# Logits of a fused attention and soft-MoE kernel as four wide products and four that add them up, with permuted features and two more weight buffers

## The chip, the cores and the metric

The kernel runs on one core of one Trainium2 chip. The metric is the device time of one execution in microseconds (us). Everything is in float32.

## The reference, cut to what matters

```python
# attention: q, k, v are (4, 8, 768, 64); 24 chunks of 32 queries; each sees 8 memory rows and up to 56 keys
for c in range(nc):
    k_full = concatenate([mem_k, k[:, :, l_start:r_end]], axis=2)     # 16 rows left of the chunk, 8 right of it
    scores = scale * matmul(q_c, k_full.T)
    a = exp(scores - max); a = a / (sum(a) + 1e-09)
    out[:, :, c_start:c_end] = matmul(a, v_full)
x = out.transpose(0, 2, 1, 3).reshape(3072, 512)                      # tokens x features
# soft MoE: 8 experts with 4 slots each, hidden size 1024
logits = x @ phi                                                      # 3072 x 32
d = softmax of logits over the tokens
slot_input = d.T @ x                                                  # 32 x 512
slot_out[e] = relu(slot_input[e] @ w1[e]) @ w2[e]
c = softmax of logits over the slots
return c @ slot_out
```

## The kernel before, in words

Attention works on 12 units (`u`) of 256 tokens, all heads. For each unit TensorE computes the scores (`s`, 64 rows of the trace: every float32 product is two), transposes the exponentials (`pt_ps`, 8), multiplies them with the values (`a`, 64), and transposes the normalized result x (`xt_ps`, 8) into xT, in which the features lie on the partitions. A loop over `i` writes the order of all engines by hand: transposes of x of unit i - 1, exponent of unit i + 1, values of unit i, scores of unit i + 2, transposes of the exponentials of unit i + 1. Two units make a group G of four 128-token blocks. In even iterations the logits of group (i - 2) / 2 follow the values: 16 products (32 rows), one for each of four feature sets of 128 (`kc`) and each of four blocks, accumulated over kc on four column groups of 32. Right behind normalizing, VectorE takes their maximum (`dispatch_max`) and ScalarE their exponential (`dispatch_exp`). In odd iterations the exponentials are transposed (`dt_ps`) and multiplied with x (`D_ps`, 8 rows of 512 columns), and VectorE adds the result to D_sb.

VectorE takes maxima, subtracts, sums and normalizes; ScalarE takes exponentials and copies transposes out of PSUM; GpSimd copies columns of k and rows of v. All loads are issued by SyncE, in program order: q two units ahead, k three buffers, v four and three buffers, and between them the experts' weights in 32 pieces of 1 MB (`load_w`). A piece goes to one of 8 buffers of its own (`w`) or to a buffer of attention that is free by then (three of k, one of q, five of v, two of x): 19 in all. `freed` lists from which half iteration each may be used. Piece i lies in buffer i modulo their number, so piece 19 waits until the experts have read piece 0.

After the loop comes a bridge of small steps: the last group's logits, the transposes of the maxima, the last D_ps, the slot inputs (`si_ps`, four products that read D_sb with a step of 4 elements, since feature p * 4 + kc belongs on partition p for w1), with filling products (`fill`) between them. Then the experts: `h` (first layer), `ht_ps`, `so` (second layer, in two halves of the output columns), `r`, and `o` (combination), whose results are copied and written out.

In front of the first scores stand 8 warming products of 128 columns, behind them 3 more.

Of the kernel before, what the change touches and what calls it, by code (L numbers as in the profile page):

```python
# [10 lines left out]
F32 = mybir.dt.float32  # L11
# [24 lines left out]
E = 8  # L36
# [16 lines left out]
WLAST = 7  # L53
WARM0 = 8
WARM1 = 3
FILL = (3, 2, 4, 1, 3, 2)
# [18 lines left out]
def tile_attn_softmoe(  # L75
# [17 lines left out]
    k_t = [cp.tile([P, 2, KW], F32, tag=f"k{i}", name=f"k{i}") for i in range(NB)]  # L93
    v_t = cp.tile([P, NE + NO, 2, VW], F32, tag="v", name="v")
    x_t = [cp.tile([P, 4, DM], F32, tag=f"x{i}", name=f"x{i}") for i in range(2)]
    w_slab = [cp.tile([P, PIECE], F32, tag=f"w{i}", name=f"w{i}") for i in range(NW)]
    lT = cp.tile([P, NG, P], F32, tag="lT", name="lT")
    late = [v_t[:, at].rearrange("p a n -> p (a n)") for at in (NE + (NU - 1) % NO, (NU - 1) % NE)]
    hT = late[0].rearrange("p (e f s) -> p e f s", e=E, s=NSLOT)
    c_sb = late[1][:, 0:4 * NG * NSLOT].rearrange("p (u s) -> p u s", s=NSLOT)  # L100
    cst = [late[1][:, 4 * NG * NSLOT + P * G:4 * NG * NSLOT + P * G + P] for G in range(NG)]
    D_sb = cp.tile([P, DM], F32, tag="D", name="D_sb")
# [42 lines left out]

    def even_v(u):

        return v_t[:, u % NE]

    def odd_v(u):  # L150
        return v_t[:, NE + u % NO]

    def load_v(u):
# [20 lines left out]
    freed += [(2 * NU - 5, q_t.rearrange("p a g n -> p (a g n)"))]  # L174
    freed += [(2 * u, even_v(u).rearrange("p a n -> p (a n)")) for u in range(NU - NE, NU - 1)]
    freed += [(2 * u, odd_v(u).rearrange("p a n -> p (a n)")) for u in range(NU - NO, NU - 1)]
    freed += [(2 * NU + d, x_t[(NG + d) % 2].rearrange("p u n -> p (u n)")) for d in range(2)]
    usable = {i: NW for i in range(2 * NU + 2)}
# [48 lines left out]
    first_k(2)  # L227
    w_ps = row(P, "warm_ps")

    def keep_warm(n, tile=None):  # L230
        for _ in range(n):
            pe.matmul(w_ps if tile is None else tile, lhsT=warm, rhs=warm, start=True, stop=True)

    keep_warm(WARM0)

    pexp, rz, xT = {}, {}, {}

# [10 lines left out]

    def scores(u, parts=1):

        if parts == 1:
            tiles = [banks(f"s{u}", "S")]
        else:
            tiles = [row(512, f"s{u}_{s}").rearrange("p (s n) -> p s n", s=1) for s in range(NSUB)]
        tiles = [t.rearrange("p s (g h n) -> p s g h n", g=NPAIR, h=2) for t in tiles]
        for s in range(NSUB):
            t, at = (tiles[0], s) if parts == 1 else (tiles[s], 0)
            for g in range(NPAIR):  # L260
                for j in range(4):
                    pe.matmul(
                        t[32 * j:32 * j + 32, at, g],
                        lhsT=q_t[:, u % NQ, g, P * s + 32 * j:P * s + 32 * j + 32],
                        rhs=key_columns(u, 4 * s + j, g),
                        start=True, stop=True,
                    )
        return tiles

    def softmax(u, tiles):  # L270
        mx = wk.tile([P, 16, 1], F32, tag="mx", name=f"mx{u}")
        p = pexp[u] = wk.tile([P, 8, 4 * CHUNK], F32, tag="p", name=f"p{u}")
        step = NSUB // len(tiles)
# [58 lines left out]
    def normalize(u, a_ps):  # L332
        dve.tensor_tensor(
            out=x_of(u).rearrange("p s (m d) -> p (s m) d", d=D),
            in0=a_ps.rearrange("p s g h d -> p (s g h) d"),
            in1=rz[u].broadcast_to([P, 16, D]),
            op=ALU.mult,
        )

    def transpose_x(u):  # L340
        for s in range(NSUB):
            t_ps = row(512, f"xt_ps{u}_{s}")
            for kc in range(NKC):
                pe.transpose(t_ps[:, P * kc:P * kc + P], x_of(u)[:, s, P * kc:P * kc + P], ident)
            xT[2 * u + s] = wk.tile([P, NKC, P], F32, tag="xT", name=f"xT{u}_{s}", bufs=4)
            act.copy(out=xT[2 * u + s].rearrange("p g n -> p (g n)"), in_=t_ps)

    def logits(G):
        l_ps = row(P, f"l{G}")
        for kc in range(NKC):  # L350
            for g in range(4):
                pe.matmul(
                    l_ps[32 * g:32 * g + 32, :],
                    lhsT=phi_sb[:, kc, :],
                    rhs=xT[4 * G + g][:, kc, :],
                    start=(kc == 0), stop=(kc == NKC - 1),
                )
        return l_ps
# [12 lines left out]
    def dispatch_exp(G, l_ps):  # L371
        d = wk.tile([P, P], F32, tag="d", name=f"d{G}")
        act.activation(out=d, in_=l_ps, func=AF.Exp, bias=nmx[G], scale=1.0, accum_out=zg[G])
        dexp[G] = d
        if G:
            act.activation(out=alpha[G], in_=nmx[G - 1], func=AF.Exp, bias=nmx[G], scale=-1.0)

    def dispatch_t(G):
        t_ps = row(P, f"dt_ps{G}")
        pe.transpose(t_ps, dexp[G], ident)  # L380
        dT[G] = wk.tile([P, P], F32, tag="dT", name=f"dT{G}")
        act.copy(out=dT[G], in_=t_ps)
# [21 lines left out]
    s0 = scores(0, 2)  # L404
    keep_warm(WARM1)
    softmax(0, s0)
# [17 lines left out]
    for i in range(NU):  # L424
# [11 lines left out]
        if G is not None and first:  # L436
            l_ps = logits(G)
        if G is not None and not first:
# [4 lines left out]
        load_w(int(WRATE * (i + 0.5)) if i < WLAST else usable[2 * i])  # L443
        if G is not None and first:
            dispatch_max(G, l_ps)
            dispatch_exp(G, l_ps)
        if G is not None and not first:
            dispatch_z(G)
            dispatch_sum(G)
        if i + 2 < NU:  # L450
            softmax(i + 2, scores(i + 2))
        if i + 1 < NU:
# [46 lines left out]
    si_ps = row(NKC * NSLOT, "si_ps").rearrange("p (c s) -> p c s", c=NKC)  # L499
    D_v = D_sb.rearrange("p (n kc) -> p kc n", kc=NKC)  # L500
    for kc in range(NKC):
# [82 lines left out]
    def expert_out(blk):  # L584
        o_ps = banks(f"so{blk}", "S")[:, 0, 0:WB]
        for e in range(E):
# [9 lines left out]
            load_w(len(slabs) + 2 * E + E * blk + e + 1)  # L596
        so = wk.tile([P, WB], F32, tag="xT", name=f"so_sb{blk}", bufs=4)
        dve.tensor_copy(out=so, in_=o_ps)
        r_ps = row(WB, f"r{blk}")
        pe.matmul(r_ps, lhsT=gsum.rearrange("p g s -> p (g s)"), rhs=so, start=True, stop=True)  # L600
        shl = wk.tile([P, WB], F32, tag="xT", name=f"shl{blk}", bufs=4)
        act.copy(out=shl, in_=r_ps)
# [41 lines left out]
def _layouts(inputs):  # L644
# [21 lines left out]

    vs = stream(v, inputs["mem_v"]).reshape(B, NPAIR, 2, STREAM, D)

# [7 lines left out]
    vw = np.stack([windows(even), windows(odd)], axis=2)  # L676
    phi = inputs["moe_phi"].reshape(NKC, P, NSLOT).transpose(1, 0, 2)
    w2 = inputs["moe_w2"].reshape(E, NFC, P, NBLK, WB).transpose(3, 0, 2, 1, 4).reshape(NBLK, E, P, PIECE)
# [20 lines left out]
```

## Time and profile before

| | us |
|---|---|
| median of 3 runs | 179.79 |
| lowest, highest | 177.65, 180.73 |
| profiled execution | 179.29 |
| its span | 177.3 |
| TensorE busy in the span | 143.3 (81%), 2679 products |
| VectorE, ScalarE, GpSimd busy | 98.3, 64.0, 31.8 |

The span reaches from the first to the last instruction; 2.0 us of the execution lie around it. 63.64 MB were moved, 359 GB/s on average. All instructions go through one helper, so they have one line (L69) and are told apart by the names of their tiles: out<-in.

### The profile page before, as it was taken

To read this page: it belongs to the slowest core of one execution; us is meant where nothing else is said; L and a number is where in the kernel's file an instruction comes from. 1 tells how busy PE (TensorE), PEld (TensorE's weight loads), DVE (VectorE), ACT (ScalarE), POOL (GpSimd) and SP (SyncE) were. 2 spreads that over 40 slices of the span, in tenths; PEclk is the share of its full clock that TensorE was granted. 3 is DMA by queue.
4 is the path that set the end of the run, shared out by engine and by line. 5 is a ranking of instruction groups with operands and counts; after the bars stand their busy time and mean duration, and the time that the engine had idled before them with its cause. 6 is when DMAs were issued, how large, how long until landed. Compare 5 with 4: busy or idle time off the path is not lost.

```text
span 177.3 us, 6114 instructions
## 1 busy us (share of the span) xinstructions
PE 143.3 (81%) x2679; PEld 111.3 (63%) x2679; DVE 98.3 (55%) x178; ACT 64.0 (36%) x123; POOL 31.8 (18%) x41
## 2 busy tenths in 40 slices
PE   7597979099949786899876939999999999799730
PEld 7485969097939576789764829767455565455420
DVE  6758879519875785479984790433056010540540
ACT  8953337106534343254270625220022220430430
POOL 8150075204134040514400000400000000000000
PEclk9879999969999999799999996999699999999985
DMA  4999977999999999999999999537599999999796
GB/s 146 309 374 409 404 289 259 334 396 407 399 383 377 363 411 412 421 409 411 424 417 366 364 403 429 159 129 237 205 381 429 418 429 414 427 407 421 323 407 255
DMA packets 12858, 63.64 MB, mean 359 GB/s; under 512 B 1952, under 2 KB 2080, under 8 KB 8352
## 3 DMA queue, kind: packets, MB, share of 16 engines
q1 hardware_dynamic: 12832, 63.25, 90.9%
q8 instruction: 21, 0.34, 0.7%
q14 instruction: 5, 0.04, 0.1%
HBM read 56.95 MB, written 6.29 MB: 357 GB/s over the span
## 4 chain that ended last, share of the span: by engine, by line
PE 65%; DMA 16%; issue 9%; DVE 4%; ACT 1%; POOL 1%; SPq 1%; DVEq 0%; POOLq 0%; ACTq 0%
PE s L69 11%; PE a L69 11%; DMA w<-in_w_dram 10%; PE h L69 9%; PE so L69 8%; PE pt_ps L69 6%; PE xt_ps L69 6%; DMA q<-in_qT_dram 4%; PE D_ps L69 3%; PE o L69 2%; PE l L69 2%; DMA k<-in_k_dram 2%; PE fill L69 1%; PE si_ps L69 1%; PE ht_ps L69 1%
## 5 line engine op out<-in xcount | busy, mean ns | idle before, releaser
L69 PE MATMUL s<-k,q 128*32 128x128 f32 x768 | 26.6, 290 | 12.7 <-DMA w<-in_w_dram 4.2
L69 PEld LDWEIGHTS s<-k,q 128*32 128x32 f32 x768 | 23.6, 117 | 16.6 <-issue 11.3
L69 PE MATMUL a<-v,pt 128*32 128x128 f32 x768 | 25.3, 279 | 4.0 <-issue 4.0
L69 ACT COPY pt<-pt_ps 128x512 f32<-128x512 f32 x24 | 13.1, 589 | 39.2 <-PE pt_ps L69 39.2
L69 POOL COPY v<-v 128x2048 f32<-128x2048 f32 x10 | 19.0, 1901 | 43.4 <-DMA v<-in_vw_dram 43.4
L69 PEld LDWEIGHTS a<-v,pt 128*32 128x32 f32 x768 | 21.0, 112 | 7.3 <-issue 6.0
L69 DVE TENSOR_TENSOR x<-a,z 128x1024 f32<-128x1024 f32 x12 | 14.7, 1224 | 10.3 <-PE a L69 9.8
L69 DVE TENSOR_REDUCE mx<-s 128x16 f32<-128x1024 f32 (+1 forms) x13 | 14.8, 1139 | 8.6 <-PE s L69 8.3
L69 PE MATMUL pt_ps<-ident,p 128*128 128x128 f32 x96 | 14.5, 294 | 3.0 <-issue 3.0
L69 PE MATMUL xt_ps<-ident,x 128*128 128x128 f32 x96 | 14.5, 297 | 2.0 <-issue 2.0
L69 DVE TENSOR_TENSOR p<-s,mx 128x512 f32<-128x512 f32 (+1 forms) x26 | 15.8, 652 | 0.4
L69 ACT COPY xT<-xt_ps 128x512 f32<-128x512 f32 x24 | 13.5, 603 | 6.7 <-PE xt_ps L69 6.7
L69 PEld LDWEIGHTS pt_ps<-ident,p 128*128 128x128 f32 x96 | 11.3, 150 | 5.6 <-issue 5.6
L69 DVE TENSOR_REDUCE z<-p 128x16 f32<-128x1024 f32 x12 | 14.6, 1219 | 0.0
L69 ACT ACTIVATE p<-p 128x1024 f32<-128x1024 f32 (+1 forms) x13 | 12.9, 994 | 4.3 <-DVE p L69 4.0
L69 PEld LDWEIGHTS xt_ps<-ident,x 128*128 128x128 f32 x96 | 12.4, 154 | 2.5 <-issue 2.5
L69 PE MATMUL o<-shl,v 32*128 32x256 f32 x96 | 7.7, 409 | 1.9 <-ACT shl L69 0.9
L69 PE MATMUL h<-w,siT 128*32 128x256 f32 x128 | 9.0, 444 | 0.0
L69 ACT ACTIVATE hs<-h,rzd 128x512 f32<-128x512 f32 x4 | 2.7, 687 | 16.0 <-PE h L69 16.0
L69 DVE COPY so_sb<-so 128x256 f32<-128x256 f32 x2 | 0.8, 424 | 13.4 <-PE so L69 13.4
L69 POOL COPY k<-k 128x192 f32<-128x192 f32 (+2 forms) x20 | 5.7, 295 | 14.3 <-DMA k<-in_k_dram 14.3
L69 PEld LDWEIGHTS o<-shl,v 32*128 32x128 f32 x96 | 5.1, 183 | 4.5 <-ACT shl L69 1.7
(97 smaller groups left out, 171.3 us busy)
## 6 DMA issues: line engine op xcount, KB each, us to landing
w<-in_w_dram SPq DMA_DIRECT2D x16, 1024.0 KB, 8.7
v<-in_w_dram SPq DMA_DIRECT2D x8, 1024.0 KB, 9.6
q<-in_qT_dram SPq DMA_DIRECT2D x12, 512.0 KB, 7.0
v<-in_vw_dram SPq DMA_DIRECT2D x20, 256.0 KB, 6.8
k<-in_w_dram SPq DMA_DIRECT2D x5, 1024.0 KB, 9.6
v<-in_vw_dram SPq DMA_DIRECT2D x20, 128.0 KB, 7.1
k<-in_k_dram SPq DMA_DIRECT2D x8, 296.0 KB, 7.2
k<-in_k_dram SPq DMA_DIRECT2D x8, 288.0 KB, 6.8
```

The source lines that it names most:

```text
L69: return self.tc.keep_in_program_order(f(*args, **kwargs))
```

## The change

- Logits of the groups 0 to 4 (the last group's stay as they were): `partial_logits` makes four products of 512 tokens, one for each feature set, each on its own 32 partitions; ScalarE copies them to SBUF (`lp`); `sum_logits` adds the four sets with four products with `sel`, between the first and the second half of the next scores. The maximum and the exponential come behind that.
- xT is one tile [128, 4, 4, 128] in place of four buffers, so that 512 tokens of a feature set are adjacent.
- Features are permuted: v's columns are reordered on the host, `normalize` writes x with the feature sets apart, in two steps of 512 elements instead of one of 1,024, and phi and the reading of D_sb follow.
- The last unit's even v buffer and the tile of the exponentials (`p`, now one tile with two halves) become weight buffers: 21 in place of 19. The small tiles that lay in the former now lie in xT. One x buffer may be used from the half iteration 22 in place of 24. `d` and `dT` have one buffer instead of two.
- Warming products have 512 columns: 2 and 1 in place of 8 and 3 of 128.

```diff
@@ -51,8 +51,8 @@
...
 WLAST = 7
-WARM0 = 8
-WARM1 = 3
+WARM0 = 2
+WARM1 = 1
 FILL = (3, 2, 4, 1, 3, 2)
@@ -92,13 +92,24 @@
...
     v_t = cp.tile([P, NE + NO, 2, VW], F32, tag="v", name="v")
+    def even_v(u):
+
+        return v_t[:, u % NE]
+
+    def odd_v(u):
+        return v_t[:, NE + u % NO]
+
     x_t = [cp.tile([P, 4, DM], F32, tag=f"x{i}", name=f"x{i}") for i in range(2)]
     w_slab = [cp.tile([P, PIECE], F32, tag=f"w{i}", name=f"w{i}") for i in range(NW)]
+    p_t = cp.tile([P, 2, 8, 4 * CHUNK], F32, tag="p", name="p")
+    xT = cp.tile([P, NKC, 4, P], F32, tag="xT", name="xT")
     lT = cp.tile([P, NG, P], F32, tag="lT", name="lT")
-    late = [v_t[:, at].rearrange("p a n -> p (a n)") for at in (NE + (NU - 1) % NO, (NU - 1) % NE)]
-    hT = late[0].rearrange("p (e f s) -> p e f s", e=E, s=NSLOT)
-    c_sb = late[1][:, 0:4 * NG * NSLOT].rearrange("p (u s) -> p u s", s=NSLOT)
-    cst = [late[1][:, 4 * NG * NSLOT + P * G:4 * NG * NSLOT + P * G + P] for G in range(NG)]
+    hT = odd_v(NU - 1).rearrange("p a (e f s) -> p (a e) f s", f=NFC, s=NSLOT)
+    small = xT.rearrange("p kc g n -> p (kc g n)")
+    n_c = 4 * NG * NSLOT
+    c_sb = small[:, 0:n_c].rearrange("p (u s) -> p u s", s=NSLOT)
+    cst = [small[:, n_c + P * G:n_c + P * G + P] for G in range(NG)]
+    rows = [small[:, at:at + WB] for at in (n_c + NG * P, n_c + NG * P + WB, 0, WB)]
     D_sb = cp.tile([P, DM], F32, tag="D", name="D_sb")
@@ -143,13 +154,6 @@
...
 
-    def even_v(u):
-
-        return v_t[:, u % NE]
-
-    def odd_v(u):
-        return v_t[:, NE + u % NO]
-
     def load_v(u):
@@ -172,9 +176,10 @@
...
     freed += [(2 * NU - 5, q_t.rearrange("p a g n -> p (a g n)"))]
-    freed += [(2 * u, even_v(u).rearrange("p a n -> p (a n)")) for u in range(NU - NE, NU - 1)]
+    freed += [(2 * u, even_v(u).rearrange("p a n -> p (a n)")) for u in range(NU - NE, NU)]
     freed += [(2 * u, odd_v(u).rearrange("p a n -> p (a n)")) for u in range(NU - NO, NU - 1)]
-    freed += [(2 * NU + d, x_t[(NG + d) % 2].rearrange("p u n -> p (u n)")) for d in range(2)]
+    freed += [(2 * NU - 3, p_t.rearrange("p a m n -> p (a m n)"))]
+    freed += [(2 * NU - 2 + 3 * d, x_t[(NG + d) % 2].rearrange("p u n -> p (u n)")) for d in range(2)]
     usable = {i: NW for i in range(2 * NU + 2)}
@@ -225,17 +230,18 @@
...
     first_k(2)
-    w_ps = row(P, "warm_ps")
-
-    def keep_warm(n, tile=None):
+    w_ps = row(512, "warm_ps")
+
+    def keep_warm(n, tile):
+        rhs = warm.rearrange("p (o n) -> p o n", o=1).broadcast_to([P, tile.shape[1] // P, P])
         for _ in range(n):
-            pe.matmul(w_ps if tile is None else tile, lhsT=warm, rhs=warm, start=True, stop=True)
-
-    keep_warm(WARM0)
-
-
-
-    pexp, rz, xT = {}, {}, {}
+            pe.matmul(tile, lhsT=warm, rhs=rhs, start=True, stop=True)
+
+    keep_warm(WARM0, w_ps)
+
+
+
+    pexp, rz = {}, {}
 
@@ -248,7 +254,7 @@
...
 
-    def scores(u, parts=1):
+    def scores(u, parts=1, between=None):
 
@@ -256,6 +262,8 @@
...
         for s in range(NSUB):
+            if s and between:
+                between()
             t, at = (tiles[0], s) if parts == 1 else (tiles[s], 0)
@@ -269,7 +277,7 @@
...
         mx = wk.tile([P, 16, 1], F32, tag="mx", name=f"mx{u}")
-        p = pexp[u] = wk.tile([P, 8, 4 * CHUNK], F32, tag="p", name=f"p{u}")
+        p = pexp[u] = p_t[:, u % 2]
         step = NSUB // len(tiles)
@@ -330,20 +338,42 @@
...
     def normalize(u, a_ps):
-        dve.tensor_tensor(
-            out=x_of(u).rearrange("p s (m d) -> p (s m) d", d=D),
-            in0=a_ps.rearrange("p s g h d -> p (s g h) d"),
-            in1=rz[u].broadcast_to([P, 16, D]),
-            op=ALU.mult,
-        )
+
+        for s in range(NSUB):
+            dve.tensor_tensor(
+                out=x_of(u)[:, s].rearrange("p (kc m d) -> p m kc d", kc=NKC, m=H),
+                in0=a_ps[:, s].rearrange("p g h (kc d) -> p (g h) kc d", kc=NKC),
+                in1=rz[u][:, H * s:H * s + H].rearrange("p m (o z) -> p m o z", z=1).broadcast_to([P, H, NKC, D // NKC]),
+                op=ALU.mult,
+            )
 
...
                 pe.transpose(t_ps[:, P * kc:P * kc + P], x_of(u)[:, s, P * kc:P * kc + P], ident)
-            xT[2 * u + s] = wk.tile([P, NKC, P], F32, tag="xT", name=f"xT{u}_{s}", bufs=4)
-            act.copy(out=xT[2 * u + s].rearrange("p g n -> p (g n)"), in_=t_ps)
+            act.copy(out=xT[:, :, 2 * (u % 2) + s, :], in_=t_ps.rearrange("p (kc n) -> p kc n", kc=NKC))
+
+    def partial_logits(G):
+
+        l_ps = row(512, f"lp{G}")
+        for kc in range(NKC):
+            pe.matmul(
+                l_ps[32 * kc:32 * kc + 32, :],
+                lhsT=phi_sb[:, kc, :],
+                rhs=xT[:, kc].rearrange("p g n -> p (g n)"),
+                start=True, stop=True,
+            )
+        lp = wk.tile([P, 512], F32, tag="lp", name=f"lp_sb{G}", bufs=1)
+        act.copy(out=lp, in_=l_ps)
+        return lp
+
+    def sum_logits(G, lp):
+        l_ps = row(P, f"l{G}")
+        for g in range(4):
+            pe.matmul(l_ps[32 * g:32 * g + 32, :], lhsT=sel, rhs=lp[:, P * g:P * g + P], start=True, stop=True)
+        dispatch_max(G, l_ps)
+        dispatch_exp(G, l_ps)
 
@@ -352,7 +382,7 @@
...
                     lhsT=phi_sb[:, kc, :],
-                    rhs=xT[4 * G + g][:, kc, :],
+                    rhs=xT[:, kc, g, :],
                     start=(kc == 0), stop=(kc == NKC - 1),
@@ -369,7 +399,7 @@
...
     def dispatch_exp(G, l_ps):
-        d = wk.tile([P, P], F32, tag="d", name=f"d{G}")
+        d = wk.tile([P, P], F32, tag="d", name=f"d{G}", bufs=1)
         act.activation(out=d, in_=l_ps, func=AF.Exp, bias=nmx[G], scale=1.0, accum_out=zg[G])
@@ -378,7 +408,7 @@
...
         pe.transpose(t_ps, dexp[G], ident)
-        dT[G] = wk.tile([P, P], F32, tag="dT", name=f"dT{G}")
+        dT[G] = wk.tile([P, P], F32, tag="dT", name=f"dT{G}", bufs=1)
         act.copy(out=dT[G], in_=t_ps)
@@ -402,7 +432,7 @@
...
     s0 = scores(0, 2)
-    keep_warm(WARM1)
+    keep_warm(WARM1, w_ps)
     softmax(0, s0)
@@ -434,21 +464,21 @@
...
         if G is not None and first:
-            l_ps = logits(G)
+            lp = partial_logits(G)
         if G is not None and not first:
...
         load_w(int(WRATE * (i + 0.5)) if i < WLAST else usable[2 * i])
-        if G is not None and first:
-            dispatch_max(G, l_ps)
-            dispatch_exp(G, l_ps)
         if G is not None and not first:
...
             dispatch_sum(G)
+        rest = (lambda: sum_logits(G, lp)) if G is not None and first else None
         if i + 2 < NU:
-            softmax(i + 2, scores(i + 2))
+            softmax(i + 2, scores(i + 2, between=rest))
+        elif rest:
+            rest()
         if i + 1 < NU:
@@ -497,7 +527,7 @@
...
     si_ps = row(NKC * NSLOT, "si_ps").rearrange("p (c s) -> p c s", c=NKC)
-    D_v = D_sb.rearrange("p (n kc) -> p kc n", kc=NKC)
+    D_v = D_sb.rearrange("p (kc n) -> p kc n", kc=NKC)
     for kc in range(NKC):
@@ -594,11 +624,10 @@
...
             load_w(len(slabs) + 2 * E + E * blk + e + 1)
-        so = wk.tile([P, WB], F32, tag="xT", name=f"so_sb{blk}", bufs=4)
+        so, shl = rows[2 * blk:2 * blk + 2]
         dve.tensor_copy(out=so, in_=o_ps)
...
         pe.matmul(r_ps, lhsT=gsum.rearrange("p g s -> p (g s)"), rhs=so, start=True, stop=True)
-        shl = wk.tile([P, WB], F32, tag="xT", name=f"shl{blk}", bufs=4)
         act.copy(out=shl, in_=r_ps)
@@ -664,7 +693,7 @@
...
 
-    vs = stream(v, inputs["mem_v"]).reshape(B, NPAIR, 2, STREAM, D)
+    vs = stream(v, inputs["mem_v"]).reshape(B, NPAIR, 2, STREAM, D // NKC, NKC).swapaxes(-1, -2).reshape(B, NPAIR, 2, STREAM, D)
 
@@ -674,7 +703,7 @@
...
     vw = np.stack([windows(even), windows(odd)], axis=2)
-    phi = inputs["moe_phi"].reshape(NKC, P, NSLOT).transpose(1, 0, 2)
+    phi = inputs["moe_phi"].reshape(P, NKC, NSLOT)
     w2 = inputs["moe_w2"].reshape(E, NFC, P, NBLK, WB).transpose(3, 0, 2, 1, 4).reshape(NBLK, E, P, PIECE)
```

## Rows read from the trace of the kernel before

**Rows 1.** The page: DMA share in 40 slices (tenths), and the instruction queue.
```profile
DMA  4999977999999999999999999537599999999796
...
q8 instruction: 21, 0.34, 0.7%
```

**Rows 2.** The chain that ended last, up to 54 us: start us, us, what.
```profile
9.64 1.58 PE warm_ps L69 x6
...
45.80 7.15 DMA q<-in_qT_dram
...
53.08 1.96 PE s L69 x64
```

**Rows 3.** The same chain, 57 to 72 us.
```profile
57.84 1.21 issue
...
69.42 2.27 issue
```

**Rows 4.** The same chain, 84 to 107 us.
```profile
84.98 0.65 PE a L69 x16
85.63 0.87 PE l L69 x32
86.50 1.75 PE s L69 x64
88.25 1.02 PE pt_ps L69 x8
89.27 0.76 PE xt_ps L69 x7
90.04 1.26 issue
91.29 0.33 PE xt_ps L69
...
91.73 1.88 PE a L69 x64
93.61 0.86 PE D_ps L69 x8
94.47 1.51 PE s L69 x52
95.99 1.65 issue
...
103.30 2.98 issue
```

**Rows 5.** Windows: stretch and its us, busy by engine, TensorE clock, DMA, GB/s.
```profile
71.70:75.90 4.20, 4.20 (x49) 3.98 (x50) 2.75 (x5) 1.30 (x3) 2.37 (x3) 0.63 1.04 424
...
106.30:111.40 5.10, 5.10 (x80) 4.67 (x83) 0.00 (x0) 2.42 (x5) 0.00 (x0) 0.67 0.97 406
```

**Rows 6.** The chain again, behind attention.
```profile
114.61 1.41 PE l L69 x32
...
120.26 2.05 PE si_ps L69 x8
...
123.45 5.28 PE h L69 x64
...
143.51 7.09 PE so L69 x128
```

**Rows 7.** Groups by shape: busy us, mean ns | idle before, and releaser.
```profile
L69 DVE TENSOR_TENSOR x<-a,z 128x1024 f32<-128x1024 f32 x12 | 14.7, 1224 | 10.3 <-PE a L69 9.8
L69 DVE TENSOR_TENSOR p<-s,mx 128x512 f32<-128x512 f32 x22 | 14.3, 694 | 0.4
L69 ACT COPY pt<-pt_ps 128x512 f32<-128x512 f32 x24 | 13.1, 589 | 39.2 <-PE pt_ps L69 39.2
L69 PEld LDWEIGHTS si_ps<-selw,D_sb 128*128 128x128 f32 x8 | 1.9, 327 | 0.2 <-DVE selw L69 0.2
L69 PEld LDWEIGHTS z_ps<-wz,gsum 128*128 128x128 f32 x2 | 0.3, 188 | 0.4 <-PE fill L69 0.4
```

## The prediction

> **What bounds the kernel now.** I read the page first. Its DMA line stands at 9 for almost the whole span, and an instruction queue moves 0.34 MB in 21 packets, which is 16 KB a packet [rows 1]. Then I read the chain that ended last, in order of time. Up to 53.08 us it is set by transfers: the scores of unit 6 start when their q lands, 7.15 us after its issue, and that q was itself issued late because the loads queue behind each other [rows 2]. From 53 us to the end of attention the chain holds no transfer at all. It holds TensorE's own work and pieces called "issue", in which TensorE waited for nothing that the trace shows [rows 3, 4].
>
> Count the products between those pieces. From 84.98 to the stall at 90.04 there are 16 + 32 + 64 + 8 + 7 = 127, from 91.29 to the stall at 95.99 there are 1 + 1 + 64 + 8 + 52 = 126 (the one dt_ps product lies between the rows at 91.29 and 91.73) [rows 4]. Every product is a weight load and a product, so a stretch is about 254 instructions; at 64 bytes an instruction, my estimate from 16 KB a packet, it is one packet of the instruction queue. So I read the stalls as TensorE running out of instructions: one packet for every 127 products or so. Work resumes at 59.05 and 71.69 [rows 3], then at 84.98, 91.29, 97.64 and 106.28 [rows 4]. From 59.05 to 71.69 and from there to 84.98 lie two packets each, so the spacings are 6.32 (twice), 6.65 (twice), 6.31, 6.35 and 8.64 us. The work of one packet takes 5.05 us (84.98 to 90.04) or 4.70 (91.29 to 95.99). So while the DMA engines are full, **TensorE gets 127 products per 6.3 us, and needs only some 5 us for them**. The long stalls cost twice: after the one of 2.27 us and the one of 2.98 us the granted clock was 0.63 and 0.67 of full speed for 4.2 and 5.1 us [rows 5], that is 1.2 GHz for most of it; 4.2 x 0.37 + 5.1 x 0.33 = 3.2 us lost.
>
> After attention the chain is a bridge of small steps and then the experts, at 55 ns a product (7.09 us for 128) with no transfer in it [rows 6]. There TensorE's work is the bound.
>
> **The change part by part.**
>
> *Logits.* A group of four 128-token blocks took 16 products in two passes, 32 rows of the trace and 0.87 us [rows 4]. Now four products of 512 tokens make 8 rows (each product is two rows). The nearest row is the D_ps step, also 8 rows of 512 columns on four column groups: 0.86 us. The four products that add the feature sets make 8 rows of 128 columns, at 27 ns (0.87 / 32) 0.22 us. So TensorE's work grows by 0.21 us a group, 1.0 us for the five groups inside attention, but 16 of its 32 rows vanish. The copy of the partial logits on ScalarE is like the pt copy, 0.59 us [rows 7]; it lies beside the first half of the next scores (0.88 us), except in iteration 10, where no scores follow and TensorE waits some 0.7 us. Without that cover it would be 0.7 us for every group, 3.5 in all.
>
> *Warming products.* 11 products, 22 rows, become 3, 6 rows, so 16 rows fewer (below, as above, a "product" of the count is a row). The second batch runs at the low clock, 1.58 us for 768 columns [rows 2]; 1,024 columns take 1.7 to 2.1, so 0.1 to 0.5 us later on the path at 11 us. The first fetches, moved by 16 products, give about as much back, and the transfer-bound stretch up to 53 us follows. I take 0 (minus 0.4 to plus 0.5).
>
> *The new places of the fetches.* Every fetch boundary now lies 16 products later for the warming and 16 more for each group done. I start both kernels at 53.08 and walk on, with s 1.75, pt 1.02, xt 0.87, dt 0.11, a 1.88, D 0.86, partial logits 0.86, sum 0.22 [rows 4] and a spacing of 6.3. The boundary before lies inside the scores of unit 6, at 54.0. The next one falls between D and the scores of unit 7: work would be there at 60.0, instructions at 60.3. Then come: 47 products into the values of unit 6 (work 65.3, instructions 66.6); 12 into the values of unit 7 (72.3, 72.9); the end of the scores of unit 9 (77.0, 79.2); the middle of the scores of unit 10 (84.9, 85.5); 6 into the scores of unit 11 (91.3, 91.8); 52 into the values of unit 10 (96.8, 98.1); 3 into the last transposes of x (7.9 us of work later, 106.0). The kernel before is at that last place 1.0 us ahead of its last logits (five transposes, four filling products and their wait), so at 114.61 - 1.0 = 113.6 [rows 6], the way from 106.28 being mostly at the lower clock [rows 5]. So the best case of this stretch is 7.6 us. Against it: the one spacing of 8.64 lay where the list of freed buffers lets six pieces of 1 MB go in three half iterations (18 to 20), and the boundary at 98.1 lies in the same part, so I put 8.6 there: plus 2.3. It then ends a stall of 3.6 us, longer than both that were followed by a lower clock, so plus 1.6 (half of 3.2). **Gain 7.6 - 2.3 - 1.6 = 3.7 us.**
>
> *The permuted features.* The four slot-input products read D_sb with a step of four elements; 8 weight loads take 327 ns each, where a load from a plain tile right behind takes 188 [rows 7]. They become plain. On the chain they take 2.05 us [rows 6], so 2.05 x 188 / 327 = 1.2: gain 0.9 (between 0 and 1.1). Normalizing becomes two VectorE steps of 512 elements; the nearest row of that size with a strided side has 694 ns, so 1.39 against 1.22 us [rows 7]. Nothing waits for it: VectorE's whole 98.3 us of busy time would be some 7 us for each of the 12 iterations with bridge and experts counted in, so I take 6.5; TensorE at 6.3 us per 127 products needs some 7.7 for the 156 of an iteration. If TensorE went faster than that, 0.2 us an iteration would show.
>
> *The bridge.* The last group's logits took 1.41 instead of 0.87 us because a boundary lay in them [rows 6, 4]; with the boundary before them: gain 0.5.
>
> *Two more buffers.* Three loads come earlier or anew: one when the last unit's probabilities are read, two in iteration 11. SyncE waits for them with only weight loads behind. The experts showed no wait for weights, so this buys nothing; it costs queue in front of the last fetches (below). Single buffers for d, dT and xT make nobody wait: each is read an iteration before it is written again.
>
> **Sum.** 3.7 + 0.9 + 0.5 = 5.1 us, from the profiled run's 179.29 (span 177.3): 174.2. The median of the three runs is 0.5 higher; I give 174.5.
>
> The Trainium skill, "Runtime: NRT & Kernel Launch", section "Instruction fetch mechanics", says that TensorE's instruction memory is refilled in 16 KiB blocks of 256 instructions and that crossing a block is mostly hidden. The block size agrees with the packets counted above; that it is hidden does not agree with stalls that stand one packet apart [rows 4].
>
> **Rivals.**
>
> *Fetches slow down with the queue.* If TensorE moves faster, the same transfers are issued closer together and every fetch waits longer: with 6.83 instead of 6.3 over the seven spacings up to 98.1, 7 x 0.53 = 3.7 us are gone, and 0.9 + 0.5 remain: 178.4 by the median. For it: 8.64 under six big transfers; the DMA line. Against it: the six other spacings lie between 6.3 and 6.7, most of them by far nearer to 6.3.
>
> *The stalls are not fetches of a fixed length.* Then fewer instructions buy nothing, and there remain 1.0 us of added products, 0.7 of waiting in iteration 10, and minus 0.9: 180.6 by the median. By the Trainium skill's rule above, "Runtime: NRT & Kernel Launch", it would be this one. Against it: 127 and 126 products.
>
> *Slower: the two added megabytes stand in front of the last two fetches.* At 424 GB/s [rows 5] 1 MB takes 2.5 us, so a spacing of 8.6 becomes 13.6. From the boundary at 100.4 the next comes at 114.0 instead of 113.6; the one after at 127.6, where work would be at 125.3. With two stretches at the lower clock: 0.4 + 2.3 + 3.2 - 1.4 = 4.5 us longer, 184.3. It decides from a spacing of about 12. Against it: the loads are issued after the first of these two fetches is asked for.
>
> **How the numbers follow.** Forecast 0.60; longer fetches 0.20; stalls that stay 0.11; slower 0.09. The forecast's own bounds: without the 8.6 and the lower clock 174.5 - 3.9 = 170.6; with both, nothing from the permutation and 0.5 from the warming, 175.9. Towards the rivals I reach to 178.6, which takes in the first; at the lower end I stop at 171.2. A change under 2% cannot be told from none here, since three runs of the kernel before lie 1.7% apart; 2% is 176.2. Faster by over 2% 0.61, within 0.30, slower 0.09.
>
> **What would show it.** Matmul rows 2,679 - 80 - 16 = 2,583 and one instruction packet less; "issue" pieces still about 127 products and 6.3 us apart, but one fewer before attention ends; the last logits starting near 110.9 instead of 114.61; si_ps near 1.2 us; the experts to the end unchanged at 53.9 us (span 177.3 less 123.45 [rows 6]). Wrong if the spacing moves off 6.3, if q of units 7 or 8 lands late, or if the lower clock comes in other stretches.

## The result, and the profile after

The changed kernel takes 171.55 us (median of 4 runs, 170.55 to 173.55) against 179.96 us (4 runs, 177.65 to 180.73) for the kernel before. The ratio is 0.9555 with a 95% interval of 0.9414 to 0.9696: faster, by 8.4 us where 5.1 were worked out. The ratio is taken over the runs within 1.5% of the fastest of their kernel, the medians over all runs. The profiled execution (170.55 us, the shortest of the four) has a span of 168.6 us, 8.7 less than before.

The page of the changed kernel: TensorE's busy time and rows, its granted clock and the DMA share in 40 slices, and the instruction queue.

```profile
PE 138.7 (82%) x2583; PEld 100.9 (60%) x2583; DVE 99.6 (59%) x190; ACT 66.2 (39%) x128; POOL 31.8 (19%) x41
...
PEclk9999999978999999999999999999999999999996
DMA  4899985999999999999999999999999999999396
...
q8 instruction: 20, 0.33, 0.8%
```

2,583 rows and one packet less, as counted. The DMA line no longer dips between attention and the experts, where it stood at 5, 3, 7, 5 [rows 1]. The clock line is lower in two slices, from 33.7 to 42.2 us (7 and 8 tenths), and at the end; the two low stretches inside attention [rows 5] are gone.

The chain of the changed kernel in order of time (start us, us, what), from the transfers to the second layer:

```profile
52.87 7.60 DMA q<-in_qT_dram
...
60.49 8.29 DMA q<-in_qT_dram
...
68.92 1.08 PE s L69 x32
...
73.54 0.67 issue
74.21 1.62 PE a L69 x52
...
78.58 0.45 issue
79.03 1.03 PE pt_ps L69 x8
...
84.80 1.76 issue
86.56 0.27 PE l L69
...
98.07 0.64 issue
98.71 0.53 PE a L69 x11
...
100.26 0.59 ACT lp_sb L69
...
108.60 1.41 PE l L69 x32
...
114.27 1.08 PE si_ps L69 x8
...
116.49 3.59 PE h L69 x64
...
134.87 7.09 PE so L69 x128
```

Read it against [rows 2, 4, 6]. Transfers of q hold the path until 68.8 us, longer than before; the scores of unit 8, which started at 68.56 us in the kernel before, start at 68.92, so that the gain lies wholly behind them. From there the issue pieces are 0.67, 0.45, 1.76 and 0.64 us, 3.5 in all. The last logits start at 108.60, not 114.61: 6.0 us. The slot-input products take 1.08, not 2.05: 1.0 us. The first h stretch takes 3.59, not 5.28: 1.7 us. That is 6.0 + 1.0 + 1.7 = 8.7 us, the whole difference of the spans.

Windows of the changed kernel (columns as in [rows 5]):

```profile
80.00:104.00 24.00, 20.90 (x435) 16.34 (x437) 18.74 (x36) 12.63 (x27) 4.29 (x4) 1.00 1.02 419
104.00:110.00 6.00, 6.00 (x119) 4.58 (x107) 2.08 (x4) 2.00 (x5) 1.81 (x1) 1.00 1.02 421
...
116.50:122.00 5.50, 5.50 (x95) 3.14 (x99) 1.44 (x4) 0.91 (x2) 0.00 (x0) 1.00 1.01 416
```

The granted clock is 1.00, that is 2.4 GHz, through the end of attention and in the first experts.

### The profile page after: what moved, and what is told of

It is laid out like the page before. It is cut to its first block, busy times and chain, and to the rows that moved or that the text cites. A ratio compares the mean times of both kernels' runs of the same rounds, so it can differ in the third digit from the quotient of the medians.

```text
span 168.6 us, 5943 instructions
## 1 busy us (share of the span) xinstructions
PE 138.7 (82%) x2583; PEld 100.9 (60%) x2583; DVE 99.6 (59%) x190; ACT 66.2 (39%) x128; POOL 31.8 (19%) x41
## 4 chain that ended last, share of the span: by engine, by line
PE 49%; DMA 34%; DVE 5%; issue 4%; ACT 2%; POOL 1%; SPq 1%; DVEq 0%; POOLq 0%; ACTq 0%
DMA q<-in_qT_dram 14%; DMA w<-in_w_dram 9%; DMA v<-in_vw_dram 9%; PE h L69 9%; PE so L69 8%; PE s L69 6%; PE a L69 6%; PE pt_ps L69 4%; PE xt_ps L69 3%; PE o L69 3%; PE D_ps L69 2%; DMA k<-in_k_dram 2%; DVE v L69 2%; PE l L69 2%; PE fill L69 1%
## 5 line engine op out<-in xcount | busy, mean ns | idle before, releaser
L69 PE MATMUL s<-k,q 128*32 128x128 f32 x768 | 26.4, 283 | 11.3 <-DMA q<-in_qT_dram 7.7
L69 PEld LDWEIGHTS s<-k,q 128*32 128x32 f32 x768 | 22.8, 113 | 19.0 <-issue 11.5
L69 DVE TENSOR_TENSOR x<-a,z 128x512 f32<-128x512 f32 x24 | 15.5, 686 | 4.0 <-PE a L69 3.2
L69 PE MATMUL pt_ps<-ident,p 128*128 128x128 f32 x96 | 13.4, 280 | 1.1 <-ACT p L69 0.6
L69 PEld LDWEIGHTS pt_ps<-ident,p 128*128 128x128 f32 x96 | 10.4, 142 | 4.4 <-issue 3.0
L69 PE MATMUL xt_ps<-ident,x 128*128 128x128 f32 x96 | 12.6, 273 | 0.0
L69 PEld LDWEIGHTS xt_ps<-ident,x 128*128 128x128 f32 x96 | 10.8, 140 | 0.1
L69 ACT ACTIVATE d<-l,stats 128x128 f32<-128x128 f32 x6 | 2.2, 368 | 18.2 <-DVE lT L69 16.3
L69 PE MATMUL o<-xT 32*128 32x256 f32 x96 | 7.7, 409 | 1.9 <-ACT xT L69 0.9
L69 DVE TENSOR_REDUCE stats<-l 128x1 f32<-128x128 f32 x6 | 1.8, 292 | 12.5 <-PE l L69 12.5
L69 DVE COPY xT<-so 128x256 f32<-128x256 f32 x2 | 0.8, 424 | 13.4 <-PE so L69 13.4
```

The costliest lines, as they stand in the source:

```text
L69: return self.tc.keep_in_program_order(f(*args, **kwargs))
```

## The experiments

Three theories. Theory 1, mine: fewer instructions, so fewer fetches that TensorE waits for. Theory 2: not the number but the place of the fetch boundaries. Theory 3: the lower clock behind long stalls, and whatever keeps it away. The four parts of the change were made alone; then the logits, the permutation and the buffers were undone one by one; then boundaries were moved without the change, and the load on the DMA engines was varied. The four kernels with one part alone keep the changed kernel's single xT tile, its tile p and the single buffers of d and dT, so they are not quite the kernel before plus one part.

For all kernels, "issue" is the sum of the issue rows in TensorE's waits between 53 and 112 us; the other columns are from the chain. All but the medians are from one profiled execution.

| kernel | median (lowest to highest), us | before in the same series | issue | last logits start | si_ps | first h |
|---|---|---|---|---|---|---|
| before | 179.96 (177.65 to 180.73) | | 10.7 | 114.61 | 2.05 | 5.28 |
| changed | 171.55 (170.55 to 173.55) | 179.96 | 3.8 | 108.60 | 1.08 | 3.59 |
| logits alone | 175.39 (172.16 to 175.67) | 178.40 | 5.0 | 110.26 | 2.05 | 5.28 |
| permutation alone | 176.83 (175.68 to 177.86) | 178.40 | 7.5 | 114.19 | 1.08 | 3.59 |
| buffers alone | 178.54 (174.12 to 180.26) | 178.40 | 10.7 | 115.77 | 2.05 | 4.93 |
| warming alone | 175.73 (174.11 to 176.22) | 178.40 | 4.5 | 110.16 | 2.05 | 4.75 |
| changed, old logits | 173.43 (171.66 to 174.35) | 178.26 | 6.3 | 109.69 | 1.08 | 3.59 |
| changed, no permutation | 173.85 (172.15 to 174.44) | 178.26 | 4.8 | 110.10 | 2.06 | 4.51 |
| changed, 19 buffers | 173.29 (171.24 to 174.42) | 178.26 | 4.5 | 109.51 | 1.08 | 3.59 |
| changed, 64 rows more | 171.98 (169.21 to 172.60) | 178.26 | 4.4 | 109.79 | 1.08 | 3.59 |
| before, 112 rows more | 177.16 (176.11 to 179.20) | 178.58 | 6.5 | 112.38 | 2.05 | 4.97 |
| before, 64 rows more | 176.53 (174.80 to 177.75) | 178.58 | 5.2 | 110.51 | 2.05 | 5.28 |
| changed, 0.8 pieces an iteration | 171.28 (169.93 to 171.63) | 178.58 | 5.6 | 108.12 | 1.08 | 3.59 |

The kernel before itself ran from 173.62 to 182.05 us in these series, so differences under 2 us are read from the profiles, not from the medians. A profile is one execution too. How far the profiles scatter can be told from kernels whose TensorE rows are the same in number and order: before, permutation alone and buffers alone have issue sums of 7.5 to 10.7 us and last logits from 114.19 to 115.77; changed, no permutation, 19 buffers and 0.8 pieces have 3.8 to 5.6 us and 108.12 to 110.10. The two groups are apart, so the number or the place of TensorE's rows shortens the stalls; a difference of 2 or 3 us of issue between two single profiles is not clear of the scatter.

The instruction queue shows that the stalls are fetches: in the trace one of its 16 KB packets starts 2.2 to 2.5 us ahead of the end of each stall. In the kernel before these packets start at 56.7, 63.1, 69.2, 82.7, 88.8, 95.1 and 104.1 us for stalls that end at 59.05, 65.47, 71.69, 84.98, 91.29, 97.64 and 106.28; in the changed kernel at 71.9, 76.7, 84.2 and 96.3 for 74.21, 79.03, 86.56 and 98.71.

**The logits alone.**

```diff
-            l_ps = logits(G)
+            lp = partial_logits(G)
...
+        rest = (lambda: sum_logits(G, lp)) if G is not None and first else None
```

> Only the logits are changed (four products of 512 tokens, a copy, four that add), with the old features, warming products and 19 buffers. Theory 1, fewer instructions: 80 of the 96 removed product rows are gone, so the issue pieces between 53 us and the end of attention shrink by some 3 to 5 us in all and the time falls to 174 to 177 us. Theory 2, place of the fetches: what counts is where the fetch boundaries fall, so the time can be anything from 173 to 181 and does not follow the number of rows. Theory 3, lower clock: the gain is the two stretches at the lower clock (3.2 us) and goes with whether a stall over 2 us is left.

175.39 us, 3.0 under the kernel before; the issue pieces fall from 10.7 to 5.0 us. That is the number of theory 1, but 64 rows more in front of the kernel before, below, bring 5.2 us, so the sum alone does not speak for fewer instructions. Its first h stretch still takes 5.28 us.

**The permutation alone.**

```diff
-    D_v = D_sb.rearrange("p (n kc) -> p kc n", kc=NKC)
+    D_v = D_sb.rearrange("p (kc n) -> p kc n", kc=NKC)
```

(with the two normalizing steps and the reordered v and phi).

> Only the features are permuted, with the old logits, warming products and 19 buffers. Theory 1: si_ps 1.1 instead of 2.05 us, so 0.9 to 1.0 us faster, 179.0 us, issue pieces as before. Theory 3: if the shorter si_ps stretch is also what keeps the full clock in the first experts, h takes 3.6 instead of 5.3 us there and the time is 177.3 us.

176.83 us, 1.6 under the kernel before. Its chain, behind attention:

```profile
119.86 1.08 PE si_ps L69 x8
...
122.08 3.59 PE h L69 x64
```

si_ps is shorter by 1.0 us, as worked out, and the first h stretch by 1.7 us, which was theory 3's point. These two places are 2.7 us of the chain; the 1.6 us of the medians are within the scatter.

**The buffers alone.**

```diff
+    freed += [(2 * NU - 3, p_t.rearrange("p a m n -> p (a m n)"))]
-    freed += [(2 * NU + d, x_t[(NG + d) % 2].rearrange("p u n -> p (u n)")) for d in range(2)]
+    freed += [(2 * NU - 2 + 3 * d, x_t[(NG + d) % 2].rearrange("p u n -> p (u n)")) for d in range(2)]
```

(and the last unit's even v buffer).

> Only the two further weight buffers and the earlier x buffer (21 pieces of 1 MB before the experts read one), all else as before. Theory 1: no product of the experts waits for a weight in the kernel before, so the same time, 179.5 to 180.5 us. Rival: the added 2 MB stand in front of the last fetches and the issue pieces grow, 181 us or more.

178.54 against 178.40: the same, as forecast, and no more issue time than the kernel before (10.7). The rival that ended on the slower side is not seen in these four runs.

**The warming products alone.**

```diff
-WARM0 = 8
-WARM1 = 3
+WARM0 = 2
+WARM1 = 1
```

> Only the warming products are changed (3 of 512 columns for 11 of 128), 16 product rows fewer, all ahead of 12 us. Theory 1: 16 rows are an eighth of a fetch block, so 0 to 0.8 us faster. Theory 2, place of the fetches: all boundaries move by 16 rows, and the time moves by 1 to 3 us in either direction.

175.73 us, 2.7 under the kernel before by the medians, for 16 rows of 2,679; but two of the seven runs of the kernel before in this series, 173.62 and 175.82, are no longer than these four. The chain of this kernel:

```profile
70.06 2.62 issue
...
85.41 0.40 issue
...
91.20 1.54 issue
...
97.66 0.27 issue
...
110.16 1.41 PE l L69 x32
...
119.22 4.75 PE h L69 x64
```

The piece of 1.65 us that stood at 95.99 [rows 4] is down to 0.27, and the one of 2.98 us at 103.30 has no successor; the last logits start 4.45 us earlier. What was changed is the number of rows, by 16, and with it the place of every boundary, and the form of the warming products. The last logits at 110.16 lie outside the 114.19 to 115.77 of the three kernels with the rows of the kernel before. By the profile theory 2 does better here than theory 1, which allowed 0.8 us; the times alone don't decide it.

**The changed kernel with the old logits.**

```diff
-            lp = partial_logits(G)
+            l_ps = logits(G)
```

> The changed kernel with the old logits (16 products a group) in all groups; permutation, buffers and warming products stay changed. Theory 1, fewer instructions: 80 product rows come back, the issue pieces between 69 us and the end of attention grow from 3.5 to 6 or 7 us, 174 to 176 us. Theory 2, place of the fetches: the time can come out on either side of the changed kernel's 171.6. Theory 3, lower clock: 171.6 unless a stall over 2 us returns, then 173 to 174.

173.43 us; issue 6.3 instead of 3.8 us, the last logits 1.1 us later. 80 rows more come with 2.5 us more of issue, as theory 1 had it, and save 1.0 us of products and 0.7 us of waiting for the copy. The time, 1.9 us longer by medians from different series, is under theory 1's 174 to 176. A stall of 2.25 us is back, and the granted clock behind it stays at 1.00 (70.9 to 75.0 us), so theory 3's price for such a stall was not paid.

**The changed kernel without the permutation.**

```diff
-    D_v = D_sb.rearrange("p (kc n) -> p kc n", kc=NKC)
+    D_v = D_sb.rearrange("p (n kc) -> p kc n", kc=NKC)
```

> The changed kernel without the permuted features: one normalizing step of 1,024 elements, D_sb read with a step of 4. If the shorter si_ps stretch keeps the full clock for the first experts: si_ps 2.05 and the first h stretch 4.7 to 5.3 instead of 3.59, together 2.3 to 2.7 us slower, 174 us. If the clock there was chance: h stays at 3.59 and only 1.0 us is lost, 172.5 us.

173.85 us. The chain of this kernel:

```profile
115.77 2.06 PE si_ps L69 x8
...
119.18 4.51 PE h L69 x64
```

1.0 + 0.9 us are back in these two places; the first h stretch is a little under the 4.7 to 5.3 us that were expected. What the longer stretch is shows a window of the kernel before, at a granted clock of 0.68 of 2.4 GHz:

```profile
123.40:128.70 5.30, 5.30 (x66) 2.66 (x65) 0.32 (x2) 0.00 (x0) 0.00 (x0) 0.68 0.52 184
```

In the kernel of this run it is 0.80:

```profile
119.20:123.70 4.50, 4.50 (x65) 2.18 (x66) 0.32 (x2) 0.00 (x0) 0.00 (x0) 0.80 0.67 231
```

Over all kernels the split is clean: first h 3.59 in all six with a short si_ps, 4.5 to 5.3 in all seven of the table with the long one. The clock there goes with the permutation and is not chance. By which of its parts, the slow weight loads or the longer stretch, no run shows.

**The changed kernel with 19 buffers.**

```diff
-    freed += [(2 * NU - 3, p_t.rearrange("p a m n -> p (a m n)"))]
```

(and the two other lines undone).

> The changed kernel with 19 buffers as before. If the two further buffers buy nothing: 171.6 us. If they are what lets the experts start at 116.5 us without waiting for weights: 13 pieces of 1 MB are left at that point instead of 11, at 420 GB/s 32.5 us, and the first output writes come among them, so the last so products wait for a weight and the time is 172.5 to 174 us.

173.29 us. TensorE's waits have a row that neither kernel has:

```profile
PE so L69 <- DMA v<-in_w_dram: 0.5, 1, 0.5
```

So once the experts start at 117 us, 19 buffers make the last so products wait for a weight: 0.5 us in this execution. SyncE's last wait, for the output, is longer as well (here, then in the changed kernel):

```profile
SPq L722 <- DMA out_dram<-x: 5.0, 1, 5.0
...
SPq L723 <- DMA out_dram<-v: 3.7, 1, 3.7
```

The span is 3.0 us longer: 0.9 are there when the first h starts (117.39 against 116.49), 0.7 more when the last so product ends, and 1.3 lie in that wait. The medians differ by 1.7 us, which is no more than the scatter.

**The changed kernel with 64 rows more in front.**

```diff
     keep_warm(WARM0, w_ps)
+    for _ in range(32):
+        pe.matmul(w_ps[0:32, 0:1], lhsT=warm[:, 0:32], rhs=warm[:, 0:1], start=True, stop=True)
```

> The changed kernel with 32 more products of 32 rows and one column (64 product rows) behind the first warming products, where TensorE waits for k anyway; they only move the fetch boundaries by half a block. Theory 1, fewer instructions: half a block more in all, ahead of the stretch that transfers bound, so 171 to 172.5 us. Theory 2, place of the fetches: the stalls fall elsewhere, and the time moves by 1.5 us or more.

171.98 us, issue 4.4 us: no effect that can be told, though the stalls lie elsewhere (the chain now goes through a wait for q until 85.0 us). This shift of the place does not matter here.

**The kernel before with 112 and with 64 rows more in front.** The same loop behind its warming products, with range(61) and WARM0 = 3, and with range(32).

> The kernel before with 112 product rows more ahead of the first scores (122 rows of 32 rows and one column, 5 warming products fewer). That moves every fetch boundary to where it lies with the changed warming products alone (16 rows fewer; 128 rows are a block), at the price of one more block. Theory 2, place of the fetches: as fast as with those, 175.7 us, the last logits starting near 110. Theory 1, number of instructions: no faster than the kernel before, 178.5 us or more, the last logits near 114.6.

> The kernel before with 64 such rows more ahead of the first scores, half a block. Theory 2, place of the fetches: the stalls of 2.27 and 2.98 us fall elsewhere and the time moves by 1.5 us or more, most likely down. Theory 1, number of instructions: within 0.8 us of the kernel before (0.8 us for a fuller clock in the first scores), 177.5 to 179 us.

177.16 us (0.993 of the kernel before, interval 0.989 to 0.997: the same, at a limit of 2%) and 176.53 us (0.987, 0.975 to 0.999: unclear). Issue falls from 10.7 to 6.5 and 5.2 us. So more instructions did not make the kernel before slower and, by intervals that end just under 1, made it slightly faster; that its boundaries lay badly explains this, and theory 1 does not. (A fuller clock in the first scores is not what helped: the scores of unit 6 start at 55.48 and 54.08 us, later than the 53.08 before.) But with the boundaries where the warming products alone put them, and one block more, the last logits start at 112.38, halfway between the 110 of theory 2 and the 114.6 of theory 1, and by the medians 112 rows gain 1.4 us, not 2.7. Neither theory alone has these numbers. That the place and the number both count fits them; what each is worth the scatter does not let one say.

**Fewer weight pieces early.**

```diff
-WRATE = 1.2
+WRATE = 0.8
```

> The changed kernel with 0.8 instead of 1.2 weight pieces an iteration up to iteration 7; the rest follows then. If the loads of q that end the waits up to 69 us are late because weight pieces lie before them, those waits shrink by 2 MB at 2.5 us less, up to 5 us, and the time falls to 167 to 170 us. If attention's end is set by the fetches alone it stays at 171.6; if the moved 2 MB are missing at the experts' end, it is 172 or more.

171.28 us, the same as the changed kernel. Its chain:

```profile
51.67 1.36 issue
...
76.72 1.26 issue
...
83.76 2.33 issue
...
108.12 1.41 PE l L69 x32
```

The wait for q at 60.49 is gone from the chain, but these issue pieces stand in its place, 5.6 us of issue in all against 3.8. So what the transfers give, the fetches take back, as far as one profile each can show it. The piece of 2.33 us, longer than one that was followed by a lower clock before, is followed by the full one:

```profile
86.10:90.00 3.90, 3.90 (x79) 3.54 (x82) 3.23 (x7) 2.62 (x8) 0.00 (x0) 1.00 1.02 422
```

**No weight piece before iteration 7, in the kernel before.**

```diff
-WRATE = 1.2
+WRATE = 0.0
```

> The kernel before with no weight piece before iteration 7, so that the DMA engines are not full until then. If a fetch takes 6.3 us because of full DMA engines, the issue pieces up to some 75 us vanish or stay under 0.5 us and come back when the pieces are issued. If a fetch takes that long anyway, issue pieces stay 127 rows and 6.3 us apart. The weights come late, so the whole time says nothing of this; 175 to 185 us.

182.29 us, of which the length says nothing. Its windows (columns as in [rows 5]):

```profile
40.00:50.00 10.00, 9.99 (x278) 8.70 (x280) 9.05 (x13) 5.08 (x9) 3.59 (x4) 1.00 0.87 289
50.00:60.00 10.00, 8.71 (x203) 6.62 (x192) 9.50 (x14) 3.79 (x9) 3.29 (x5) 1.00 0.84 283
60.00:70.00 10.00, 9.37 (x198) 7.95 (x201) 9.60 (x16) 4.68 (x11) 2.37 (x3) 1.00 0.77 233
70.00:80.00 10.00, 9.38 (x260) 8.14 (x259) 9.67 (x13) 5.09 (x10) 3.16 (x4) 1.00 0.84 297
```

With DMA shares of 0.77 to 0.87 there is not one issue piece, through six packets of the instruction queue; the chain runs along VectorE there, busy for 9.05 to 9.67 of 10 us. A slower TensorE could hide the fetches, so the times at which they start decide. In the kernel before, the next packet starts 3.7 to 4.1 us after a stall ends, and once 6.5 us, ahead of the stall of 2.98. Here, counting rows to the same boundaries, it starts 0.7 to 2.3 us after each boundary that TensorE passes from 43 to 74 us, and 3.5 to 4.0 us after the next two, when the weight pieces have been issued (from 73.0 us on). An idle time of 11.3 us, booked as issue, ends at 99.5; the q that is needed then was issued at 80.70 behind eight weight pieces, so I read it as a wait for q. The stalls come with full DMA engines, not with a fetch as such: in these stretches a fetch comes some 2 us later with full engines.

## Why the prediction was right, and where its steps were off

**The bound and the places: right.** The walk put boundaries 12 rows into the values of unit 7, at the end of the scores of unit 9, in the sum inside the scores of unit 10, and 52 rows into the values of unit 10. The stalls of the changed kernel are 9 rows into the first, 63 of 64 into the second, behind row 6 of the sum, and 50 into the last. That the stalls are fetch boundaries is shown by this and by the packets that start 2.2 to 2.5 us ahead of each stall's end; that full DMA engines make them long, by the kernel without early weights.

**The spacing: the term that was mis-sized.** I took 6.3 us for every block and 8.6 once, and one stretch at the lower clock. Resumptions at 74.21, 79.03, 86.56 and 98.71 give 4.82, 7.53 and twice 6.08 us; the 8.6 and the lower clock did not come. Stalls of over 2 us, behind which the clock fell before, are missing. Against this the wait for q until 68.8 us cost 1.0 us, which I had named as what could go wrong (the scores of unit 8 start at 68.92; by the walk at 66.6 + 0.5 + 0.86 = 68.0). Net: 6.0 us where I had 3.7, inside the step's best case of 7.6. That a long stall brings the lower clock was in the prediction from two cases, and the runs do not bear it out: behind 2.33 us (0.8 pieces), 2.25 (old logits) and 2.67 (112 rows more) the clock stayed at 1.00, behind 2.04 (19 buffers) it was 0.57 for 4.0 us and behind 1.91 (permutation alone) 0.63 for 4.2 us.

**The warming products: sized in the wrong place.** I put them at 0, from the path at 11 us, and let their 16 rows move every boundary of the walk without a price of their own. Alone they gave 2.7 us by the medians, which the scatter leaves uncertain. The low clock that I took for the second batch did not come: from 6 to 15 us the granted clock was 1.00, where it was 0.81 in the kernel before.

**The permutation: right for si_ps, one consequence missed.** 2.05 to 1.08 us, forecast 1.2. That the shorter stretch would keep the clock at 2.4 GHz for the first experts, 1.7 us, was nowhere in the sum. Two normalizing steps: 686 ns each, forecast 694, and TensorE waited for none from 53 us on. The reason given for that rests on too small a number, 6.5 us of VectorE an iteration: in the kernel without early weights, where the chain runs along VectorE, its normalizing steps start 7.2 to 7.8 us apart (51 to 82 us), about the 7.7 us that TensorE was given. So there was hardly any slack.

**The bridge: wrong.** The last logits take 1.41 us in both kernels and in every variant. It was no fetch: in the changed kernel the weight loads pause after six because the second xT copy on ScalarE ends at 108.88, 0.3 us behind the first product. The 0.5 us were not there to be gained.

**The logits: right in the small terms.** The copy takes 586 ns and TensorE waits for it once, in iteration 10 (98.71 to 100.90 in the chain). Each sum stands where the first half of the scores ends.

**The buffers: right alone, incomplete in the whole.** They gain nothing on the kernel before; with the experts 7 us earlier, 19 buffers bring the wait of 0.5 us, and in the one profile an output that lands 1.3 us later.

**The rivals.** Longer fetches with a fuller queue: there in the one spacing of 7.53 us, and in the variant with fewer early pieces, where fetches took back what q gave, but not as a loss here. Stalls that are not fetches of a fixed length: fetches they are, by the packets; of a fixed length they are not (4.82 to 7.53 us), and still the time fell. That fewer instructions as such shorten the stalls is likely and not shown apart from the place: issue fell to 5.0 us with 80 rows fewer (logits alone) and to 5.2 with 64 rows more. The two added megabytes as a loss: not seen with the buffers alone. The Trainium skill's "Runtime: NRT & Kernel Launch", section "Instruction fetch mechanics", calls the crossing of a block mostly hidden; the runs agree at DMA shares up to 0.87 and disagree when the engines are full (stalls of 0.45 to 1.76 us in the changed kernel, up to 2.98 in the one before).

**How much was luck.** The measured 171.55 us lie 0.35 us above the lower end of the range. The 3.9 us of costs for a long spacing and the lower clock did not come, and 1.7 us of clock came that the sum did not hold; against them stand the wait for q, 1.0 us, and the missing 0.5 of the bridge. Without these two the time would have been about 170, below the range, so that it lies inside is partly luck. (The forecast's last step is loose too: 174.2 and 0.5 are 174.7, not 174.5.)

Open: what makes a spacing 4.8 us once and 7.5 the next time (the packet starts 2.5 us after 74.21 and 5.2 us after 79.03), at which instruction a fetch is asked for, and how the 6.0 us divide between fewer rows and better places. The kernel before varies by 8 us from run to run, and a profile shows one execution.

## What to carry to other kernels

When TensorE idles for "issue" at equal counts of instructions while the DMA engines are full, count rows between the stalls and look for packets of the instruction queue just ahead of their ends: fewer and longer instructions, or less transfer at that time, can help, and a few instructions more or fewer in front move the stalls. Try such a shift as a control before a gain is put down to the edit itself. Where variants leave an engine's instructions as they are, use them as repeats to see how far single profiles scatter. Look at what a small stretch does to the clock of the large one behind it, and at whether a buffer that buys nothing today is needed once the rest is faster.

## What the runs showed of the hardware that was not expected

A fetch of instructions came late when the DMA engines were full: the next packet started 3.7 to 6.5 us after a stall's end in the kernel before, and 0.7 to 2.3 us after a boundary at DMA shares of 0.77 to 0.87. Sixteen rows fewer in front went with a median 2.7 us lower and last logits 4.45 us earlier, and adding 64 or 112 rows of TensorE work to the kernel before did not make it slower (0.987 and 0.993). The clock behind a stall was not set by the stall's length: 1.00 behind 2.67 us (112 rows more in the kernel before), 0.57 behind 2.04 us (19 buffers):

```profile
74.40:79.00 4.60, 4.59 (x100) 4.10 (x100) 3.58 (x5) 2.96 (x5) 2.37 (x3) 1.00 1.01 399
...
79.50:83.50 4.00, 4.00 (x36) 3.67 (x39) 2.33 (x5) 2.27 (x5) 1.63 (x3) 0.57 1.01 415
```

A weight load of 128 columns read with a step of four elements took 327 ns where the plain one takes 191:

```profile
L69 PEld LDWEIGHTS si_ps<-selw,D_sb 128*128 128x128 f32 x8 | 1.0, 191 | 0.2 <-DVE selw L69 0.2
```

And a stretch of such slow loads, 1 us longer, went with a first h stretch of 4.5 to 5.3 us in every kernel that had it, where it took 3.59 us at a granted clock of 1.00 in the changed kernel.
